# Moving a kernel's weight loads from the SyncE queue into the casting GpSimd queue, with the order of all engines planned anew

## The chip, the cores and the metric

One Trainium2 chip, one of its cores. Times are device microseconds (us) of that core; a kernel is run several times and the median is told. "Fast" runs are those in the undisturbed state. Medians here are over all runs; ratios use the fast runs alone. A profile of one execution goes with every kernel; its span is some 1.8 us below the measured time, because it leaves out start and end.

## The reference

Two parts in a row, for 8 batches of 576 tokens. First an attention with 8 heads of 64, whose keys and values are averages over 8 tokens (so 72 of them). Then four "expert" attentions with causal masks on its output `x`; a gate picks two experts for each token.

```python
# attention, for each batch and head (scale = 1/8 in both parts)
k_p = k.reshape(B, H, 72, 8, 64).mean(axis=3);  v_p = the same of v
x = softmax(scale * q @ k_p.T) @ v_p            # heads side by side: 576 x 512
# experts e = 0..3, weights wq, wk, wv: 512 x 64 each, wo: 64 x 512, w_gate: 512 x 4
logits = x @ w_gate                             # the best two of four, softmax over these two
qe, ke, ve = x @ wq[e], x @ wk[e], x @ wv[e]
ye = softmax(causal(scale * qe @ ke.T)) @ ve @ wo[e]
out += gate_weight[e] * ye                      # out: 8 x 576 x 512, fp32
```

Inputs are fp32; the kernel computes in bf16. q, k and v are 28.3 MB, the weights 2.1 MB, and the output 9.4 MB.

## The kernel before

The kernel is a list of small units (load a piece, transpose q, scores, ...), written out in one planned order, `SEQ`. A token names a unit, its step and its batch: `L` loads, `Pk`, `Pv`, `Pt` pool k and v, `Q` transposes q, `E` makes scores, `N` multiplies with v, `X` transposes x (all of the first attention); `q`, `k`, `v` project, `g` gates, `s` makes scores, `o` multiplies with v, `T` transposes and `y` projects out (experts). Each engine does its share of the list strictly in this order; only semaphores make it wait. So an engine whose next unit lacks its data waits, even if a later unit could run.

All loads of q, k and v (11 per batch) are issued by GpSimd and turn fp32 into bf16 on the way. The weights come as fp32 on SyncE's queue, and VectorE and ScalarE cast them:

```python
def load_weights():                                    # token W:0
    ...                                                # fp32 tiles wst_q, wst_k, wst_v, wst_g, wst_o
    for nm in ("q", "k", "v", "g", "o"):
        nc.gpsimd.memset(wst[nm][one element], 0.0)    # GpSimd releases SyncE at this place of the order
    for nm, src in (("q", moe_wq), ("k", moe_wk), ("v", moe_wv)):
        nc.sync.dma_start(out=wst[nm], in_=src, 128 partitions x 16 pieces of 64 elements)
    nc.sync.dma_start(out=wst["g"], ...); nc.sync.dma_start(out=wst["o"], ...)

def cast_weights(step):                                # tokens c0..c3
    if step < 2:      # q, k:  two nc.vector.tensor_copy each, fp32 -> bf16, reordered for two experts side by side
    elif step == 2:   # v and gate: two nc.vector.tensor_copy into wvg
    else:             # output weights: two nc.scalar.copy

SEQ = """
  L1:0 L9:0 L2:0 L7:0 L6:0 L4:0 M:0 L8:0 L5:0 L0:0 L3:0 L10:0 L8:1 L0:2
  I:0 Q0:0 Pk:0 Pv:0 Pt:0 L2:1 L0:1 Q1:0 ...          # I: the masks that Pk needs
  L3:2 X3:0 N1:1 E0:1 L6:2 N2:1 X1:1 L7:2 L4:2 N0:1 Pk:2 E3:1 W:0 X2:0
  L9:2 L8:2 Q1:2 Pt:2 Q2:2 Q0:2 L10:2 N3:1 E1:2 L0:3 E0:2 L3:4 E2:2 c0:0
  Q3:2 X2:1 X0:1 L2:3 X3:1 L1:3 q00:0 ...              # first projection: batch 2's attention half done
```

The softmax here doesn't subtract the row's maximum and nothing guards it: scores larger than these inputs give would overflow.

## Time and profile before

196.41 us (three runs, 195.08 to 196.64) when the prediction was made; 195.75 to 197.14 as the median of the later calls.

How to read it: TensorE (PE) is the engine with the most work. Its time is its busy time plus its idle time, so the question is where it idles. From the busy times by stretch:

| profile before, us | before 60 us | from 60 us to the last matmul | last matmul to the end | whole span |
|---|---|---|---|---|
| length | 60.0 | 125.9 | 7.5 | 193.4 |
| TensorE busy | 36.2 | 123.1 | 0 | 159.2 |
| TensorE idle | 23.8 | 2.8 | 7.5 | 34.2 |

What TensorE waited for between 25 and 60 us, in the list of waits (total us, times, longest):

```profile
PE vg_ps L319 <- DVE wvg L190: 3.5, 1, 3.5
PE qT_ps L238 <- DMA qraw_84<-in_q_dram: 2.9, 1, 2.9
PE kp_ps L387 <- DVE wkp_114 L181: 1.6, 1, 1.6
```

Two of the three are waits for weights: `wvg` and `wkp` are VectorE's cast copies. The third is batch 2's q data. And the weights' own transfers (KB, us from issue to landing), and the SyncE sequencer that issued them (start, length of the record):

```profile
wst_q<-in_moe_wq_dram SPq DMA_DIRECT2D x1, 512.0 KB, 10.5
wst_k<-in_moe_wk_dram SPq DMA_DIRECT2D x1, 512.0 KB, 16.6
wst_v<-in_moe_wv_dram SPq DMA_DIRECT2D x1, 512.0 KB, 17.9
wst_g<-in_moe_w_gate_dram SPq DMA_DIRECT2D x1, 8.0 KB, 13.0
```
```profile
27.57 0.44 SPq L165 DMA_DIRECT2D wst_q<-in_moe_wq_dram  x1
28.06 4.52 SPq L165 DMA_DIRECT2D wst_k<-in_moe_wk_dram  x1
32.62 5.69 SPq L165 DMA_DIRECT2D wst_v<-in_moe_wv_dram  x1
38.36 6.48 SPq L169 DMA_DIRECT2D wst_g<-in_moe_w_gate_dram  x1
44.88 1.19 SPq L172 DMA_DIRECT2D wst_o<-in_moe_wo_dram  x1
```

The gate weights, 8 KB, are issued last but one and land at 38.36 + 13.0 = 51.4 us; only then can the first value projection start.

### The profile page before, as it was taken

Reading aid. Unit: us, or ns where it says so; the run is one execution under the profiler, and the core shown is the slowest. Engines: PE = TensorE matmul, PEld = TensorE weight load, DVE = VectorE, ACT = ScalarE, POOL = GpSimd, SP = SyncE. Lnnn points to the kernel's source line nnn. Section 1 sums busy time; section 2 is a strip of 40 time slices with the busy share of each in tenths; the row PEclk is TensorE's granted clock in tenths of the full one; section 3 lists DMA queues with packets and bytes.
Section 4 is the critical chain, followed back from the end, with each engine's and each line's share of the span. In section 5 each row is a group of like instructions: output and inputs, shape, how many; then the busy total and the mean of one; then the engine's idle time right before and its main releaser. Section 6 shows DMA issues by size and latency. Waiting matters only on the chain.

```text
span 193.4 us, 5522 instructions
## 1 busy us (share of the span) xinstructions
PE 159.2 (82%) x2136; PEld 112.4 (58%) x2147; DVE 145.1 (75%) x558; ACT 123.9 (64%) x276; POOL 100.0 (52%) x173
## 2 busy tenths in 40 slices
PE   0009896796299999999999999999999999999940
PEld 0006463484267768685786676676777687756510
DVE  7005698675399989997799889698879877798900
ACT  2001866242666997459956968978988653989532
POOL 7999997430458799389695624010423210444000
PEclk9999999789999999999999999999999999999996
DMA  4999999999999999999999999630004110046565
GB/s 42 151 169 180 160 178 163 170 168 167 209 110 131 105 138 141 163 221 183 121 134 198 166 105 125 206 107 32 3 0 162 60 31 3 2 183 216 168 229 191
DMA packets 87404, 26.08 MB, mean 135 GB/s; under 512 B 82512, under 2 KB 82512, under 8 KB 87376
## 3 DMA queue, kind: packets, MB, share of 16 engines
q0 software_dynamic: 75136, 14.16, 88.6%
q1 hardware_dynamic: 12240, 11.55, 21.1%
q8 instruction: 17, 0.28, 0.5%
q14 instruction: 11, 0.09, 0.2%
HBM read 30.42 MB, written 9.44 MB: 206 GB/s over the span
## 4 chain that ended last, share of the span: by engine, by line
PE 44%; POOL 17%; DMA 13%; DVE 10%; ACT 7%; SPq 5%; issue 2%; DVEq 0%; POOLq 0%; ACTq 0%
DMA wst_g<-in_moe_w_gate_dram 7%; PE vg_ps L319 6%; PE oB_ps L458 6%; PE kp_ps L387 5%; SPq L165 5%; PE y_ps L500 5%; PE qp_ps L387 5%; DMA qraw_83<-in_q_dram 4%; PE sB_ps L411 4%; POOL qraw_83 L151 3%; PE xT_ps L304 3%; POOL qraw_82 L151 3%; PE oA_ps L281 2%; POOL qraw_84 L151 2%; DMA out_dram<-ofin 2%; PE sA_ps L255 2%
## 5 line engine op out<-in xcount | busy, mean ns | idle before, releaser
L442 POOL TENSOR_SCALAR_AFFINE_SELECT etb_93<-etb_93 128x256 bf16<-128x256 bf16 x32 | 12.7, 417 | 31.8 <-ACT etb_93 L429 31.8
L442 POOL TENSOR_SCALAR_AFFINE_SELECT etb_94<-etb_94 128x256 bf16<-128x256 bf16 x32 | 12.8, 416 | 30.2 <-ACT etb_94 L429 30.2
L293 DVE TENSOR_TENSOR x_tm<-oA_ps,rz 128x320 bf16<-128x320 f32 x64 | 28.2, 482 | 0.0
L429 ACT ACTIVATE etb_93<-sB_ps 128x512 bf16<-128x512 f32 x48 | 25.7, 620 | 1.3 <-PE sB_ps L411 1.3
L429 ACT ACTIVATE etb_94<-sB_ps 128x512 bf16<-128x512 f32 x48 | 25.1, 626 | 0.5 <-PE sB_ps L411 0.5
L509 ACT COPY ofin<-y_ps 128x512 f32<-128x512 f32 (+1 forms) x32 | 18.1, 597 | 10.9 <-DMA out_dram<-ofin 3.6
L270 ACT ACTIVATE eta_91<-sA_ps 96x512 bf16<-96x512 f32 x32 | 17.0, 620 | 7.8 <-PE sA_ps L255 7.8
L244 DVE COPY qT<-qT_ps 128x576 bf16<-128x576 bf16 x32 | 13.8, 451 | 6.5 <-PE qT_ps L238 5.9
L270 ACT ACTIVATE eta_92<-sA_ps 96x512 bf16<-96x512 f32 x32 | 16.6, 604 | 1.6 <-PE sA_ps L255 1.6
L151 POOL DMA_DIRECT2D qraw_82<-in_q_dram x15 | 12.9, 868 | 5.9 <-DMA vraw_90<-in_v_dram 4.6
L213 ACT CAST kp<-kp_ps 96x512 bf16<-96x512 f32 x8 | 4.8, 597 | 17.0 <-PE kp_ps L201 17.0
L304 PE MATMUL xT_ps<-ident,x_tm 128*128 128x128 bf16 x160 | 14.2, 225 | 0.7 <-DVE x_tm L293 0.5
L477 DVE TENSOR_TENSOR o_sc<-oB_ps,gt 128x320 bf16<-128x320 f32 x32 | 14.2, 484 | 0.3 <-PE oT_ps L487 0.3
L255 PE MATMUL sA_ps<-qT,kpT 64*96 64x512 bf16 (+1 forms) x128 | 14.2, 314 | 0.0
L151 POOL DMA_DIRECT2D qraw_83<-in_q_dram x15 | 12.9, 873 | 0.1
L394 ACT CAST qTB<-qp_ps 128x288 bf16<-128x288 f32 x17 | 6.8, 423 | 9.2 <-PE qp_ps L387 9.0
L304 PEld LDWEIGHTS <-x_tm 128*128 128x128 bf16 x160 | 10.8, 101 | 2.8 <-DVE x_tm L293 1.4
L319 PE MATMUL vg_ps<-wvg,xT_103 128*128 128x260 bf16 x60 | 8.4, 274 | 3.5 <-DVE wvg L190 3.5
L129 PE MATMUL one_ps<-ones,pool_111 96*32 96x8 bf16 x3 | 0.2, 188 | 12.5 <-POOL pool_111 L117 12.5
L290 DVE RECIPROCAL rz<-oA_ps 128x5 f32<-128x5 f32 x64 | 8.8, 174 | 2.1 <-PE oA_ps L281 2.0
L326 DVE CAST vaug_100<-vg_ps 128x256 bf16<-128x256 f32 x20 | 8.3, 418 | 1.7 <-PE vg_ps L319 1.7
L458 PE MATMUL oB_ps<-vaug_100,etb_94 128*128 128x65 bf16 x240 | 9.2, 193 | 0.1
(200 smaller groups left out, 441.4 us busy)
## 6 DMA issues: line engine op xcount, KB each, us to landing
out_dram<-ofin SPq DMA_DIRECT2D x32, 256.0 KB, 3.0
kraw_85<-in_k_dram POOLq DMA_DIRECT2D x9, 192.0 KB, 6.0
vraw_88<-in_v_dram POOLq DMA_DIRECT2D x9, 192.0 KB, 5.1
vraw_89<-in_v_dram POOLq DMA_DIRECT2D x9, 192.0 KB, 6.0
kraw_86<-in_k_dram POOLq DMA_DIRECT2D x9, 192.0 KB, 5.4
qraw_82<-in_q_dram POOLq DMA_DIRECT2D x12, 128.0 KB, 5.8
qraw_83<-in_q_dram POOLq DMA_DIRECT2D x12, 128.0 KB, 6.4
kraw_87<-in_k_dram POOLq DMA_DIRECT2D x6, 192.0 KB, 6.1
```

Source lines behind the costliest of these rows:

```text
L151: nc.gpsimd.dma_start(out=dst, in_=src)
L255: nc.tensor.matmul(out=s_ps[hh][:, 64 * i : 64 * i + 64] if tail else s_ps[hh][:], lhsT=kpT[r0 : r0 + D, i, :], rhs=st["qT", i][r0 : r0 + ...
L270: nc.scalar.activation(out=eta[:, hp, hh, 0:512], in_=s_ps[hh][:], func=EXP, scale=ATT_EXP_SCALE)
L293: nc.vector.tensor_tensor(out=x_tm[:, :, h * D : (h + 1) * D], in0=o_ps[hh][:, :, 0:D], in1=rz[:, hh].to_broadcast([128, NTC, D]), op=MULT,)
L304: nc.tensor.transpose(out=x_ps[:, c * 128 : (c + 1) * 128], in_=x_tm[:, c, fc * 128 : (fc + 1) * 128], identity=ident[:, :],)
L319: nc.tensor.matmul(out=vg_ps[:], lhsT=xT[:, fc, tc_ * 128 : (tc_ + 1) * 128], rhs=wvg[:, fc, :], start=(fc == 0), stop=(fc == NFC - 1),)
L387: nc.tensor.matmul(out=p_ps[:], lhsT=wqk[nm, ep][:, fc, :], rhs=xT[:, fc, cols], start=(fc == 0), stop=(fc == NFC - 1),)
L429: nc.scalar.activation(out=et[:, ep, e, eo : eo + off], in_=s_ps[e][:, 0:off], func=EXP, scale=MOE_EXP_SCALE)
L442: nc.gpsimd.affine_select(out=blk, in_=blk, pattern=[[0, 2], [1, 128]], compare_op=ISGE, fill=0.0, base=0, channel_multiplier=-1,)
L458: nc.tensor.matmul(out=o_ps[e][:, qc, :], lhsT=et[:, ep, e, col : col + 128], rhs=vaug[:, kc, 2 * ep + e, :], start=(kc == 0), stop=(kc == ...
L477: nc.vector.tensor_tensor(out=o_sc[:, :, e * HD : (e + 1) * HD], in0=o_ps[e][:, :, 0:HD], in1=gt[:, e].to_broadcast([128, NTC, HD]), op=MULT,)
L509: copy(out=ofin[0:nrows, :], in_=y_ps[0:nrows, :])
```

## The change

Its intent: the weights stand in the same GpSimd queue as the activations, behind exactly the two batches that TensorE needs first; they arrive as bf16, so VectorE only puts them in order; and the list of units is planned anew around this.

```diff
-    wop = [const.tile([128, DM], BF16, name=f"wop{ep}") for ep in range(NEP)]
+    wop = const.tile([128, NEP, DM], BF16, name="wop")
-    def load_weights():            # fp32, SyncE, released by five memsets on GpSimd
-        ...
+    wst = {nm: stp.tile([128, E, NFC, HD], BF16, ...) for nm in ("q", "k", "v")}
+    def load_weights(st, i):       # tokens W0..W4: q, k, v, gate, output weights
+        ...
+        nc.gpsimd.dma_start(out=dst, in_=src)          # fp32 -> bf16 in flight
+    def order_weights(st, i):      # tokens c0..c2: the same VectorE copies, now bf16 -> bf16; no ScalarE copies
 SEQ:
-        L1:0 L9:0 L2:0 L7:0 L6:0 L4:0 M:0 L8:0 L5:0 L0:0 L3:0 L10:0 L8:1 L0:2
-        I:0 Q0:0 Pk:0 Pv:0 Pt:0 L2:1 L0:1 Q1:0 ...
+        L2:0 L8:0 L10:0 L1:0 L6:0 L0:0 L5:0 L7:0 L3:0 L4:0 L9:0 M:0 I:0 Pk:0
+        Pt:0 Q0:0 Q1:0 Q2:0 Q3:0 E0:0 L0:1 Pv:0 L2:1 L6:1 L1:1 L3:1 E2:0 L7:1
+        E4:0 E1:0 E3:0 N2:0 L4:1 N0:0 Pk:1 L5:1 L9:1 X2:0 L8:1 L10:1 X0:0 N3:0
+        Pt:1 W0:0 W1:0 Q0:1 W2:0 W3:0 Q2:1 Q3:1 Q1:1 E0:1 X3:0 N1:0 E4:1 E3:1
+        L7:2 E1:1 Pv:1 E2:1 X1:0 c0:0 N0:1 N3:1 c1:0 N1:1 q10:0 c2:0 L2:2 L1:2
+        ...                        # first projection after batch 0 and most of batch 1; W4 much later; all the rest reordered
```

More of the change, by code (lines that the diff above doesn't have):

```diff
@@ L151, in load, with load_weights, order_weights @@
         nc.gpsimd.dma_start(out=dst, in_=src)
-    wst = {}
-    def load_weights():
-        for nm in ("q", "k", "v"):
-            wst[nm] = stp.tile([128, E, NFC, HD], FP32, name=f"wst_{nm}")
-        wst["g"] = stp.tile([128, NFC, E], FP32, name="wst_g")
-        wst["o"] = stp.tile([128, NEP, DM], FP32, name="wst_o")
-        for nm in ("q", "k", "v", "g", "o"):
-            nc.gpsimd.memset(wst[nm][0:1, 0, 0:1] if nm in "go" else wst[nm][0:1, 0, 0, 0:1], 0.0)
-        for nm, src in (("q", moe_wq), ("k", moe_wk), ("v", moe_wv)):
-            nc.sync.dma_start(
-                out=wst[nm][:].rearrange("p e fc d -> p (e fc) d"),
-                in_=src.rearrange("e (fc p) d -> p (e fc) d", p=128),
-            )
-        nc.sync.dma_start(
-            out=wst["g"][:], in_=moe_w_gate[:, :].rearrange("(fc p) e -> p fc e", p=128)
-        )
-        nc.sync.dma_start(
-            out=wst["o"][:],
-            in_=moe_wo.rearrange("e d n -> (e d) n").rearrange("(ep p) n -> p ep n", p=128),
-        )
-    def cast_weights(step: int):
-        if step < 2:
-            nm = "qk"[step]
+    wst = {nm: stp.tile([128, E, NFC, HD], BF16, name=f"wst_{nm}") for nm in ("q", "k", "v")}
+    wst_g = stp.tile([128, NFC, E], BF16, name="wst_g")
+    def load_weights(st, i: int):
+        if i < 3:
+            dst = wst["qkv"[i]][:].rearrange("p e fc d -> p (e fc) d")
+            src = (moe_wq, moe_wk, moe_wv)[i].rearrange("e (fc p) d -> p (e fc) d", p=128)
+        elif i == 3:
+            dst, src = wst_g[:], moe_w_gate.rearrange("(fc p) e -> p fc e", p=128)
+        else:
+            dst = wop[:]
+            src = moe_wo.rearrange("e d n -> (e d) n").rearrange("(ep p) n -> p ep n", p=128)
+        nc.gpsimd.dma_start(out=dst, in_=src)
+    def order_weights(st, i: int):
+        if i < 2:
+            nm = "qk"[i]
             for ep in range(NEP):
@@ L184, in cast_weights @@
                 )
-        elif step == 2:
+        else:
             nc.vector.tensor_copy(
@@ L189, in cast_weights @@
             )
-            nc.vector.tensor_copy(out=wvg[:, :, E * HD : VG], in_=wst["g"][:])
-        else:
-            for ep in range(NEP):
-                nc.scalar.copy(out=wop[ep][:], in_=wst["o"][:, ep, :])
+            nc.vector.tensor_copy(out=wvg[:, :, E * HD : VG], in_=wst_g[:])
     def pool_half(raw, nm: str):
@@ L502, in wo_out @@
                 lhsT=st["oT", ep][:, qc * 128 : (qc + 1) * 128],
-                rhs=wop[ep][:],
+                rhs=wop[:, ep, :],
                 start=(ep == 0),
@@ L516 @@
     UNITS = {
-        "L": load, "I": setup_consts, "M": setup_pads, "W": load_weights,
+        "L": load, "I": setup_consts, "M": setup_pads, "W": load_weights, "c": order_weights,
         "Pk": pool_k, "Pv": pool_v, "Pt": pool_kT, "Q": q_transposes, "E": scores_a, "N": av_a,
@@ L522 @@
     SEQ = """
-        L1:0 L9:0 L2:0 L7:0 L6:0 L4:0 M:0 L8:0 L5:0 L0:0 L3:0 L10:0 L8:1 L0:2
-        I:0 Q0:0 Pk:0 Pv:0 Pt:0 L2:1 L0:1 Q1:0 Q2:0 L1:1 Q3:0 L3:1 E0:0 L6:1
-        L4:1 E4:0 E2:0 L7:1 E1:0 N0:0 Pk:1 N2:0 L5:1 N1:0 X0:0 Pt:1 E3:0 X1:0
-        Q3:1 Q1:1 L9:1 Q0:1 L10:1 Q2:1 N3:0 E1:1 Pv:1 E4:1 L1:2 L2:2 E2:1 L5:2
-        L3:2 X3:0 N1:1 E0:1 L6:2 N2:1 X1:1 L7:2 L4:2 N0:1 Pk:2 E3:1 W:0 X2:0
-        L9:2 L8:2 Q1:2 Pt:2 Q2:2 Q0:2 L10:2 N3:1 E1:2 L0:3 E0:2 L3:4 E2:2 c0:0
-        Q3:2 X2:1 X0:1 L2:3 X3:1 L1:3 q00:0 q10d:0 L5:3 q11d:0 q01d:0 c1:0 q00d:1 q01d:1
@@ L530 @@
-        q10:1 k00d:0 k01d:0 k10d:1 k10:0 L7:3 L6:3 E4:2 L4:3 c2:0 s01:0 L3:3 E3:2 s00:0
-        v0:0 v1:0 v2:0 k11d:0 v3:0 L9:4 v4:0 s20:0 g0:0 L6:4 g1:0 L9:3 L10:3 s02:0
-        s11:0 s10:0 g2:0 Pv:2 L8:3 v0:1 v1:1 N3:2 N1:2 k00:1 L2:4 g3:0 k01:1 N0:2
-        q11:1 N2:2 L5:5 k11:1 X3:2 Pk:3 s01:1 s12:0 X1:2 L4:4 L7:4 g4:0 v2:1 L5:4
-        Pt:3 L1:5 X2:2 L10:4 v3:1 Q2:3 s20:1 g5:0 L4:5 s02:1 g6:0 g7:0 g8:0 s11:1
-        L1:4 s00:1 Q0:3 Q3:3 v4:1 X0:2 o00:0 Q1:3 L0:4 o01:0 k00d:2 c3:0 k10:2 E4:3
@@ L536 @@
-        E0:3 g0:1 s10:1 o10:0 o11:0 L8:5 q10d:2 Pv:3 E2:3 g1:1 E1:3 E3:3 T1:0 v0:2
-        v1:2 T0:0 k01d:2 N2:3 g2:1 N0:3 L4:6 L7:5 q00:2 g3:1 N3:3 k11:2 L0:5 Q0:4
-        Q2:4 L2:5 L10:5 q11:2 N1:3 L8:4 v2:2 X2:3 X3:3 y1:0 y0:0 v3:2 Pk:4 g4:1
-        s12:1 L3:6 g5:1 s12:2 g6:1 v4:2 L6:5 L5:6 g7:1 X0:3 y3:0 Q3:4 y2:0 g8:1
-        g0:2 Pt:4 o00:1 L3:5 Q1:4 g1:2 X1:3 L2:6 o10:1 o01:1 L6:6 o11:1 L1:6 E4:4
-        s11:2 Pk:5 g2:2 Pv:4 s10:2 E1:4 q01d:2 v0:3 v1:3 T1:1 L3:7 s02:2 E0:4 s00:2
-        v2:3 L9:5 g3:2 q10:3 g4:2 N1:4 g5:2 q00:3 g6:2 Q3:5 v3:3 q01:3 s20:2 L10:7
@@ L543 @@
-        s01:2 E2:4 g7:2 E3:4 L0:6 T0:1 X1:4 v4:3 Q2:5 L8:7 L5:7 g8:2 N0:4 Q0:5
-        k10d:3 N2:4 k11:3 q11:3 N3:4 y1:1 L7:7 o10:2 L7:6 Pt:5 o11:2 y0:1 L8:6 L4:7
-        Q1:5 y4:0 o00:2 L2:7 o01:2 g0:3 X3:4 Pk:6 Pv:5 L6:7 s12:3 g1:3 g2:3 E2:5
-        s11:3 X0:4 k00d:3 X2:4 T0:2 L10:6 Pt:6 k01d:3 k00:4 E4:5 E0:5 g3:3 g4:3 L1:7
-        E3:5 E1:5 Q1:6 L9:7 v0:4 Q0:6 v1:4 Q1:7 Q2:6 Q3:7 v2:4 s20:3 E0:6 s10:3
-        N1:5 T1:2 L0:7 v3:4 g5:3 N0:5 L9:6 v4:4 q10d:4 N2:5 y2:1 g6:3 y1:2 y3:1
-        q11:4 Q0:7 g0:4 s01:3 g1:4 s00:3 E1:6 Q3:6 X2:5 Q2:7 X1:5 y2:2 g7:3 N3:5
@@ L550 @@
-        k10d:4 y4:2 X0:5 k01:4 E4:6 g2:4 E3:6 g3:4 E2:6 s02:3 Pk:7 g8:3 Pv:6 Pv:7
-        o10:3 g4:4 o11:3 X3:5 y4:1 y0:2 N1:6 Pt:7 y3:2 N2:6 k11d:4 q00:4 k00:5 N0:6
-        k01:5 E3:7 E1:7 s10:4 q01d:4 N3:6 q00d:5 o00:3 o01:3 s00:4 s01:4 q10d:5 X1:6 v0:5
-        v1:5 E4:7 s12:4 s20:4 T0:3 X3:6 g5:4 k10:5 N1:7 q11:5 s02:4 E2:7 g6:4 E0:7
-        q01d:5 X2:6 v2:5 X1:7 v3:5 T1:3 X0:6 k11:5 N3:7 s00:5 s01:5 s12:5 y2d:3 y1d:3
-        q10:6 N0:7 v4:5 k00d:6 X3:7 y0:3 q11d:6 g0:5 g1:5 s20:5 g2:5 g3:5 s11:4 s02:5
@@ L556 @@
-        k01d:6 N2:7 o00:4 k10:6 y3:3 g7:4 g8:4 o01:4 g4:5 X0:7 X2:7 q00d:6 q01:6 s11:5
-        s10:5 y4:3 g5:5 q00:7 o00:5 q01:7 g6:5 T0:4 k10:7 g7:5 g8:5 o01:5 o10:4 o11:4
-        o10:5 k00d:7 k01:7 q10d:7 o11:5 v0:6 T1:4 k11d:7 q11:7 v0:7 v1:7 s00:6 s00:7 s01:7
-        v2:7 T0:5 v1:6 v3:7 s10:7 s12:7 s11:7 T1:5 k11d:6 v2:6 v3:6 y3d:5 v4:7 g0:7
-        y1d:5 s20:6 s20:7 s02:7 v4:6 g1:7 g0:6 y1d:4 g2:7 g1:6 g3:7 g4:7 y2:5 y4d:5
-        g2:6 s10:6 g5:7 g6:7 g7:7 s11:6 s12:6 g3:6 g4:6 g8:7 y0:5 o10:7 o11:7 o00:7
@@ L562 @@
-        o01:7 y0:4 y3:4 s02:6 s01:6 y2d:4 g5:6 T0:7 g6:6 T1:7 o10:6 g7:6 g8:6 o11:6
-        y4:4 y1:7 o00:6 o01:6 y4:7 y0:7 T1:6 y2:7 T0:6 y3d:7 y2:6 y0:6 y1:6 y3:6
-        y4:6
+        L2:0 L8:0 L10:0 L1:0 L6:0 L0:0 L5:0 L7:0 L3:0 L4:0 L9:0 M:0 I:0 Pk:0
[3 more added lines that the diff above has]
+        L7:2 E1:1 Pv:1 E2:1 X1:0 c0:0 N0:1 N3:1 c1:0 N1:1 q10:0 c2:0 L2:2 L1:2
@@ new lines @@
+        q00:0 L0:2 N2:1 q01:0 X0:1 X3:1 L4:2 L5:2 q11:0 k00:0 L6:2 k10:0 k01:0 k11:0
+        L3:2 v0:0 v1:0 L10:2 s20:0 s02:0 L8:2 s12:0 s11:0 X1:1 v2:0 v3:0 L7:3 v4:0
+        L9:2 X2:1 L2:3 Pk:2 s10:0 s01:0 g0:0 g1:0 s00:0 q00:1 v0:1 g2:0 Pt:2 L1:3
+        g3:0 L0:3 L4:3 Q2:2 L3:3 g4:0 v1:1 Q1:2 k00:1 Q0:2 L6:3 L5:4 L5:3 Q3:2
+        L8:3 g5:0 g6:0 q10:1 v2:1 E4:2 E2:2 g7:0 E1:2 E3:2 Pv:2 v3:1 v4:1 N2:2
+        L9:3 q01:1 N1:2 k01:1 Pk:3 E0:2 L7:4 s00:1 g8:0 s02:1 g0:1 L4:4 L10:3 X2:2
+        L1:4 k10d:1 N3:2 q11:1 g1:1 X1:2 N0:2 k11:1 L10:4 o00:0 o10:0 L0:4 X3:2 Pt:3
@@ new lines @@
+        L2:4 Q0:3 L6:4 X0:2 o11:0 g2:1 o01:0 L3:4 Q1:3 L7:5 Q3:3 v0:2 q10:2 L6:5
+        k10:2 q00d:2 k00:2 W4:0 T0:0 s20:1 s12:1 s11:1 Q2:3 q11d:2 v1:2 L2:5 v2:2 E4:3
+        E3:3 L4:5 E0:3 s10:1 Pv:3 Pk:4 v3:2 T1:0 L1:5 v4:2 N0:3 g0:2 q01:2 L5:5
+        Q3:4 g3:1 k01:2 L0:5 s01:1 L3:5 L8:4 E2:3 E1:3 L9:4 g4:1 g5:1 g1:2 Q0:4
+        Q2:4 g6:1 y4:0 X0:3 Pt:4 Q1:4 L9:5 N2:3 k11:2 L10:5 y0:0 N1:3 E4:4 s02:2
+        X2:3 N3:3 g7:1 g2:2 o00:1 g8:1 o10:1 L2:6 L3:6 X1:3 y2:0 o01:1 E3:4 L4:6
+        E2:4 L7:6 o11:1 Q3:5 L8:5 X3:3 Q1:5 Pk:5 L5:6 Pv:4 L6:6 s10:2 s00:2 L1:6
@@ new lines @@
+        E0:4 v0:3 y3d:0 Q2:5 g3:2 v1:3 q00d:3 L0:6 T1:1 L8:6 v2:3 v3:3 L10:6 s11:2
+        s12:2 E1:4 L9:6 Pt:5 k00d:3 N0:4 q10:3 y1:0 L1:7 g4:2 T0:1 N2:4 g5:2 v4:3
+        g6:2 E1:5 E2:5 X0:4 y1:1 L9:7 Q2:6 Q0:5 Q3:6 k01:3 X2:4 N3:4 k10:3 L0:7
+        L7:7 Q0:6 N1:4 s20:2 E4:5 g7:2 g0:3 g8:2 L10:7 Pk:6 Pv:5 E0:5 s01:2 E3:5
+        X1:4 Q1:6 L5:7 L2:7 g1:3 q01:3 Pt:6 N2:5 y2:1 g2:3 X3:4 k11:3 g3:3 N0:5
+        g4:3 q11:3 X2:5 E4:6 E1:6 E3:6 L6:7 N1:5 o00:2 o01:2 q10:4 X1:5 o10:2 k10:4
+        o11:2 s20:3 g5:3 L4:7 s12:3 s01:3 v0:4 N3:5 y4:1 X0:5 T1:2 L3:7 v1:4 s10:3
@@ new lines @@
+        s11:3 s00:3 T0:2 k11:4 g6:3 v2:4 y0:1 g7:3 X3:5 v3:4 Pv:6 Pk:7 s02:3 E2:6
+        L8:7 E0:6 q11:4 q00d:5 Q1:7 v4:4 g0:4 Q3:7 N3:6 q00:4 g8:3 N2:6 y3:1 o10:3
+        q01:4 o00:3 o01:3 Pt:7 k00:5 o11:3 y4:2 X2:6 g1:4 k00:4 k01d:4 N1:6 y1:2 Q2:7
+        s10:4 E1:7 N0:6 Q0:7 X3:6 q10:5 k10:5 X1:6 E4:7 s01:4 E2:7 g2:4 s02:4 g3:4
+        Pv:7 X0:6 T0:3 v0:5 y2d:2 T1:3 q01:5 v1:5 s11:4 s12:4 g4:4 E3:7 v2:5 g5:4
+        g6:4 k01:5 N1:7 v3:5 y1d:3 g7:4 v4:5 y3:2 k11:5 s20:4 g0:5 E0:7 s00:4 g1:5
@@ new lines @@
+        s01:5 q10d:6 q11:6 q11d:5 k00d:6 g2:5 N3:7 q00:6 N0:7 y3d:3 y4d:3 y2:3 k10:6 o10:4
+        g8:4 o00:4 g3:5 N2:7 o11:4 q01:6 o01:4 y0:2 v0:6 s02:5 s10:5 y0d:3 k11:6 T0:4
+        v1:6 s11:5 s00:5 s12:5 X3:7 g4:5 T1:4 v2:6 k01:6 g5:5 v3:6 X1:7 g6:5 g7:5
+        y4:4 v4:6 y1:4 y2:4 g0:6 X2:7 g1:6 X0:7 g2:6 s20:5 g8:5 s02:6 s12:6 s10:6
+        o00:5 k00:7 g3:6 y3d:4 o01:5 o10:5 o11:5 g4:6 k10:7 q00:7 v0:7 s01:6 s11:6 s00:6
+        g5:6 v1:7 v2:7 v3:7 T0:5 q01d:7 v4:7 k01:7 q10d:7 T1:5 s20:6 s01:7 g0:7 s02:7
@@ L565 @@
+        s00:7 o00:6 g6:6 g1:7 g7:6 g8:6 g2:7 g3:7 o01:6 q11:7 g4:7 o10:6 g5:7 g6:7
+        o11:6 k11:7 y3:5 y0d:4 s20:7 s11:7 g7:7 s12:7 s10:7 y1d:5 g8:7 T1:6 T0:6 y4d:5
+        y2:5 o00:7 y1:6 o01:7 y0:6 o10:7 o11:7 y4:6 y0:5 y2:6 T0:7 T1:7 y3:6 y2:7
+        y0:7 y1:7 y3:7 y4:7
     """
@@ L576 @@
             copy = nc.vector.tensor_copy if on_dve else nc.scalar.copy
-            if name in "IMW":
+            if name in "IM":
                 UNITS[name]()
-            elif name == "c":
-                cast_weights(int(digits))
             elif name == "L":
```

## The prediction

> **What bounds the kernel now.** The profile's first part gives TensorE 159.2 us busy of a 193.4 us span. The busy times by stretch put its 34.2 us of idleness in three places: 23.8 us in the first 60 us (14.3 of them before 20 us), 2.5 us between 60 and 180 us, 7.8 us after 180 us. In the middle TensorE is 98% busy, so nothing but less TensorE idleness at the two ends can help much. The timeline shows the head: the first matmul on q data waits until 14.5 us; batch 0 and 1 then run until about 35 us with gaps for data; the first projection starts at 40.1 us; the key projection waits for its weights until 45.3 us and the value projection until 51.9 us (the waits list has VectorE waiting 2.1 us for the k weights and 3.2 us for v; TensorE then waits 1.6 and 3.5 us for VectorE's casts). The weights were asked for only at 27.6 us, on the SyncE queue, and took 10.5, 16.6 and 17.9 us from issue to landing for 512 KB each, gate 13.0 us, in competition with the activation loads. The DMA row is full and the rate some 170 GB/s (counted in bf16) from 5 to 50 us, so the loads are limited by rate there, not by latency.
>
> **What the change does.** The four projection weights enter the casting GpSimd queue after exactly two batches of loads (22 transfers), and batch 2, of which the old order had already issued much, comes after them. Trainium skill, "DMA: Bandwidth & Descriptors", section "SWDGE vs HWDGE vs iDMA": only the GpSimd path casts in flight; so half the bytes land, and VectorE only reorders bf16. The same page ("Issuing engines are not separate DMA queues") says all issuers share the 16 engines: the gain is order, not a new path. Removed: five tiny memsets, two 0.69 us ScalarE casts, none critical. Added on GpSimd: five issues; from 0.69, 0.77 and 0.88 us for 512, 768 and 1024 pieces I estimate 1.3 us for a 2048-piece weight, 5 us in all. VectorE's five or six reorderings stay near 0.4 us each. TensorE's work is unchanged.
>
> **Estimate.** Two batches are 3.54 MB as bf16: at 170 GB/s, landed at about 25 us; q, k, v, gate weights (0.79 MB) by about 30-31 us instead of 50.6. GpSimd's masks come after 11 issues instead of 13, and pooled k is first on TensorE, so it starts near 11.5 us. Before the first projection the new order has only batches 0 and 1 of attention, some 14 us of TensorE work; the first projection should start near 30 us, so about 16 us idle by then. After it, the rest of both batches (about 30 us of work) covers batch 2's loads. With 2 to 3 us of small stalls the first 60 us cost 18 to 19 us of idleness instead of 23.8. The middle and the tail (still 11 stores bunched behind four output buffers, 7.5 us after the last matmul) I expect unchanged within 1.5 us. Gain about 5.5 us: 191 us, range 187 to 194.8. Chances: faster by over 2% 0.68, within 2% 0.28, slower 0.04.
>
> **Signs.** Right: value projection starts at 32-36 us; weight waits gone; TensorE idle under 20 us in the first 60; TensorE busy sum within 1.5 us of 159; tail 7 to 8 us. Wrong step: weight landings after 36 us, or batch 1 data late by as much.
>
> **What would make it wrong.** The 128-byte weight pieces moving well below 170 GB/s; the new order stalling TensorE in mid-kernel (idle 60-180 us above 5 us); a longer tail; or batch 2's data arriving after the covering work is used up.

## More of the kernel before

The stretches from which the head is read (columns: start and end, length, busy us and instructions of PE, PEld, DVE, ACT and POOL, the TensorE clock that was granted, as a share of full speed, the DMA share, which is the summed time of the packets over that of 16 engines and passes 1 where packets overlap, and GB/s):

```profile
0.00:60.00 60.00, 36.16 (x423) 24.42 (x424) 35.47 (x128) 24.29 (x52) 41.42 (x67) 0.97 1.68 155
30.00:35.00 5.00, 2.12 (x30) 1.24 (x29) 3.00 (x11) 2.24 (x5) 3.87 (x5) 1.00 1.84 166
35.00:40.00 5.00, 4.72 (x52) 3.63 (x53) 4.19 (x12) 2.47 (x6) 1.69 (x3) 0.66 1.49 171
45.00:50.00 5.00, 3.08 (x32) 1.94 (x32) 2.43 (x7) 2.54 (x7) 0.54 (x2) 1.00 1.60 165
```

TensorE works only 2.12 of the 5 us from 30 us; just after this its granted clock is 0.66. DMA moves 165 GB/s (counted as it lands, in bf16 where cast) all the time.

## The result, and the profile after

183.99 us (four runs, 183.62 to 185.82) beside 195.75 us before. The ratio is 0.9427 (95% interval 0.933 to 0.952); ratios here are the mean time of one kernel's fast runs over that of the other's of the same rounds, so not quite the ratio of the medians. A later repeat of the same kernel (e14) gave 184.05 us and 0.9344. The gain is 11.8 us, about twice the predicted 5.5, and the time lies below the predicted range.

The stretches of the new kernel:

```profile
0.00:60.00 60.00, 43.38 (x569) 30.75 (x570) 39.51 (x159) 31.44 (x71) 50.41 (x75) 1.00 1.75 138
30.00:35.00 5.00, 4.90 (x76) 4.08 (x74) 4.97 (x21) 3.61 (x9) 2.79 (x4) 1.00 2.24 165
35.00:40.00 5.00, 5.00 (x56) 3.85 (x54) 4.13 (x15) 3.98 (x12) 2.51 (x6) 1.00 1.65 121
45.00:50.00 5.00, 4.83 (x64) 3.22 (x62) 3.86 (x16) 4.20 (x11) 5.00 (x7) 1.00 1.69 161
```

From 30 us on TensorE hardly idles, and the dip of its clock is gone. The waits for weights are gone from the list of waits between 25 and 60 us; the largest that is left:

```profile
PE sA_ps L244 <- DVE qT L233: 0.6, 1, 0.6
```

And the weights, whose GpSimd issues start at 21.2 us:

```profile
wst_q<-in_moe_wq_dram POOLq DMA_DIRECT2D x1, 256.0 KB, 8.0
wst_k<-in_moe_wk_dram POOLq DMA_DIRECT2D x1, 256.0 KB, 8.5
wst_v<-in_moe_wv_dram POOLq DMA_DIRECT2D x1, 256.0 KB, 9.7
wst_g<-in_moe_w_gate_dram POOLq DMA_DIRECT2D x1, 4.0 KB, 8.9
```

The gate weights are there at 24.58 + 8.9 = 33.5 us instead of 51.4. Up to 30 us nothing was gained (TensorE idle 15.5 us before, 15.8 after); the head's whole gain lies between 30 and 60 us. Where TensorE's time went, in the profiled executions (a matmul count below 2147 means that records are missing from that trace, and the busy time is then a little too low and the idle time too high):

| us | span | busy | matmuls seen | idle before 60 | idle 60 to last matmul | last matmul to end |
|---|---|---|---|---|---|---|
| before | 193.4 | 159.2 | 2136 | 23.8 | 2.8 | 7.5 |
| after | 181.9 | 157.0 | 2130 | 16.6 | 1.5 | 6.8 |
| after, repeat (e14) | 181.4 | 158.5 | 2147 | 15.6 | 0.6 | 6.8 |
| e1: old order, casting queue | 186.4 | 159.3 | 2147 | 17.3 | 3.1 | 6.7 |
| e3: new order, SyncE queue | 193.5 | 162.9 | 2147 | 22.2 | 0.9 | 7.5 |
| e4: new order, weights late | 192.9 | 162.4 | 2147 | 21.9 | 1.6 | 7.0 |

Between before and the repeat, which has all its records: 8.2 us less idle in the head, 2.2 in the middle, 0.7 in the tail, and 0.8 busy; 12.0 us together. The head is most of it.

### The profile page after: what moved, and what is told of

It reads as the page before. It is cut to its first block, busy times and chain, and to the rows that moved or that the text cites. A ratio compares the mean times of both kernels' runs of the same rounds, so it can differ in the third digit from the quotient of the medians.

```text
span 181.9 us, 5531 instructions
## 1 busy us (share of the span) xinstructions
PE 157.0 (86%) x2130; PEld 111.5 (61%) x2147; DVE 137.0 (75%) x541; ACT 128.9 (71%) x291; POOL 105.2 (58%) x173
## 4 chain that ended last, share of the span: by engine, by line
PE 62%; DMA 12%; POOL 10%; ACT 9%; DVE 4%; issue 2%; ACTq 0%; POOLq 0%
PE oB_ps L447 8%; PE vg_ps L308 7%; PE kp_ps L376 7%; PE qp_ps L376 7%; PE y_ps L489 6%; PE sB_ps L400 5%; PE oA_ps L270 4%; PE xT_ps L293 4%; DMA qraw_82<-in_q_dram 4%; PE sA_ps L244 4%; PE qT_ps L227 4%; DMA kraw_86<-in_k_dram 3%; DMA kraw_85<-in_k_dram 3%; ACT etb_93 L418 3%; POOL qraw_82 L151 2%; POOL kraw_85 L151 2%
## 5 line engine op out<-in xcount | busy, mean ns | idle before, releaser
L418 ACT ACTIVATE etb_93<-sB_ps 128x512 bf16<-128x512 f32 x48 | 25.0, 613 | 2.1 <-PE sB_ps L400 2.0
L418 ACT ACTIVATE etb_94<-sB_ps 128x512 bf16<-128x512 f32 x48 | 25.0, 622 | 0.4 <-PE sB_ps L400 0.4
L383 ACT CAST qTB<-qp_ps 128x288 bf16<-128x288 f32 x24 | 9.9, 418 | 8.0 <-PE qp_ps L376 7.7
L244 PE MATMUL sA_ps<-qT,kpT 64*96 64x64 bf16 (+1 forms) x128 | 13.7, 312 | 0.6 <-DVE qT L233 0.6
L151 POOL DMA_DIRECT2D qraw_83<-in_q_dram x15 | 12.8, 866 | 0.3 <-issue 0.3
L151 POOL DMA_DIRECT2D qraw_82<-in_q_dram x15 | 12.8, 870 | 0.0
L151 POOL DMA_DIRECT2D qraw_84<-in_q_dram x10 | 8.8, 887 | 3.2 <-DMA wst_v<-in_moe_wv_dram 1.4
L447 PEld LDWEIGHTS <-etb_94 128*128 128x128 bf16 x240 | 8.7, 97 | 2.2 <-issue 0.6
```

The costliest lines, as they stand in the source:

```text
L151: nc.gpsimd.dma_start(out=dst, in_=src)
L244: nc.tensor.matmul(out=s_ps[hh][:, 64 * i : 64 * i + 64] if tail else s_ps[hh][:], lhsT=kpT[r0 : r0 + D, i, :], rhs=st["qT", i][r0 : r0 + ...
L418: nc.scalar.activation(out=et[:, ep, e, eo : eo + off], in_=s_ps[e][:, 0:off], func=EXP, scale=MOE_EXP_SCALE)
L447: nc.tensor.matmul(out=o_ps[e][:, qc, :], lhsT=et[:, ep, e, col : col + 128], rhs=vaug[:, kc, 2 * ep + e, :], start=(kc == 0), stop=(kc == ...
```

## The experiments

Sixteen runs were made, e1 to e16, all with correct results. The theories: *arrival* (the gain is the earlier arrival of the weights), *order* (the replanned order makes it, the path is only its vehicle), and within arrival *queue* (which queue the weights stand in) against *cast* (half the bytes, cheaper reorderings); later also *clock* (gaps cost a slow stretch after them).

**e1: the old order, only the weight path changed.**

```diff
 (the new kernel's code, with the old SEQ:)
-  ... Pk:2 E3:1 W:0 X2:0 ...
+  ... Pk:2 E3:1 W0:0 W1:0 W2:0 W3:0 W4:0 X2:0 ...      and without c3:0
```

> Old written order, only the weight path changed: the five weight transfers go through the casting GpSimd queue at the very place where the old order asked SyncE for them (27.6 us), bf16 reorderings in place of casts. Arrival theory (the gain is the weights' arrival, whatever brings it): q, k, v, gate land at about 35, 36, 38, 38 us instead of 38, 45, 50 and 51; the waits of 1.6 us (k) and 3.5 us (v) on TensorE vanish; time 190 to 191.5 us, about 5 us under the old kernel. Order theory (the replanned order makes the gain, the path is only its vehicle): within 2 us of the old kernel.

Measured: 187.91 us beside 196.4, ratio 0.955; again as e15 187.52 us, 0.9495. So the path alone, at the old place, gives 8.5 to 9.6 us. The arrival theory holds, and I had the size of this too low as well. Both waits for weights vanished; the wait for batch 2's q data fell from 2.9 to 1.5 us too, and is now the largest between 25 and 60 us:

```profile
PE qT_ps L227 <- DMA qraw<-in_q_dram: 1.5, 1, 1.5
```

3.5 + 1.6 + 1.4 = 6.5 us, and idle before 60 us fell by as much, from 23.8 to 17.3. (The two profiled spans differ by 7.0 us, 0.9 of it in the tail; the rest of the 8.5 us lies in the spread between runs.)

**e2: the same, with the four projection weights moved forward to the new kernel's place in the queue.**

```diff
-  ... L10:1 ...      ... W0:0 W1:0 W2:0 W3:0 W4:0 ...
+  ... L10:1 W0:0 W1:0 W2:0 W3:0 ...     ... W4:0 ...
```

> As the run before, and the q, k, v and gate weights are moved forward to just behind batch 1's last load (about 21 us), the place they have in the new kernel; everything else in the old order. TensorE's old order does nearly all of batch 2's attention before the first projection, and batch 2's data now comes some 4.5 us later. Arrival theory: weights land by 31 us, but TensorE then waits for batch 2's q data (2.9 us already in the old trace), so no better than the run before, 190 to 193 us: early weights are worth something only if TensorE's order uses them. Order theory in its strict form: no gain over the old kernel.

Measured: 194.46 us, ratio 0.990, just above the 190 to 193 that the arrival theory expected. Earlier weights are 6.5 us slower than later ones here: TensorE's old order wants batch 2's attention before the first projection, and batch 2 now stands behind the weights. TensorE's two largest waits between 25 and 60 us are for its data:

```profile
PE kp_ps L190 <- DMA kraw<-in_k_dram: 2.5, 1, 2.5
PE qT_ps L227 <- DMA qraw<-in_q_dram: 1.4, 1, 1.4
```

In 35 to 45 us the granted clock is 0.50 and 0.64.

**e3: the new order, with the old fp32 path on SyncE.**

```diff
-  ... Pt:1 W0:0 W1:0 Q0:1 W2:0 W3:0 ...   ... W4:0 ...
+  ... Pt:1 W:0 Q0:1 ...                   ... c3:0 ...       old load_weights and cast_weights
```

> New written order on all engines, old weight path: fp32 through SyncE asked for at the place of the new kernel's first weight transfer (about 21 us), with the old casts on VectorE and ScalarE. Arrival theory: from the old 10.5, 16.6 and 17.9 us to landing and the serial issue on SyncE, q lands at about 32, k at 38, v at 44 us; TensorE idles some 6 to 8 us more than in the new kernel before 60 us: 190 to 192 us. Order theory: at most 186 us.

Measured: 195.88 us beside 196.4, ratio 0.9989 (0.992 to 1.006). The new order alone is worth nothing. The weights landed as expected (31.8, 37.4 and 43.4 us), yet the time is 4 us above the expected 190 to 192; the profile shows TensorE 4.4 us busier than in the new kernel's repeat, in part in stretches of half clock. Its first projections come where the weights are not yet there; the two largest waits between 12 and 60 us:

```profile
PE vg_ps L319 <- DVE wvg L190: 4.8, 1, 4.8
PE qp_ps L387 <- DVE wqp L181: 2.9, 1, 2.9
```

**e4: the new kernel with batch 2's eleven loads in front of the weights.**

```diff
-  ... Pt:1 W0:0 W1:0 ...
+  ... Pt:1 L7:2 L2:2 L1:2 L0:2 L4:2 L5:2 L6:2 L3:2 L10:2 L8:2 L9:2 W0:0 W1:0 ...
```

> The new kernel with batch 2's eleven loads moved in front of the weights in the GpSimd queue; nothing else changes. Arrival theory: 1.77 MB more at about 165 GB/s ahead of the weights, so they land some 10 us later (39 to 44 us instead of 29 to 33.5), and TensorE's order has nothing to do in between: idle up to 9 us more in the first 60 us, 191 to 193 us. Order theory: 184 to 186 us.

Measured: 193.38 us, ratio 0.986, against 191 to 193 expected. Same path, same cast, same order on TensorE, VectorE and ScalarE: only the weights' place in GpSimd's queue, behind batch 2's loads, differs, and 9.4 of the 11.8 us are lost. TensorE waits 8.1 us for the q weights. Together, e1 to e4 show that place and order must fit each other.

**e5: the old kernel, its fp32 weights issued by GpSimd instead of SyncE.** No cast in flight, same place, same casts on VectorE and ScalarE.

```diff
-            nc.sync.dma_start(out=wst[nm], ...)
+            nc.gpsimd.dma_start(out=wst[nm], ...)            (all five)
```

> The old kernel with one change: its five fp32 weight transfers are issued by GpSimd instead of SyncE, at the same place, without a cast in flight; the old casts on VectorE and ScalarE stay. Tells the queue from the cast. If the gain of the first run (old order, casting queue: 187.9 us) comes from the weights standing in line in the one GpSimd queue instead of sharing the engines piecewise from a second queue: 187.5 to 189.5 us. If it comes from the halved bytes and cheaper reorderings: 192 us or more.

Measured: 187.81 us beside 196.6, ratio 0.952 (one of the four runs, 190.08 us, is slow; the median of the other three is 187.25). One word, the issuing engine, makes the whole gain of e1. The transfers and their issue:

```profile
wst_k<-in_moe_wk_dram POOLq DMA_DIRECT2D x1, 512.0 KB, 8.9
wst_v<-in_moe_wv_dram POOLq DMA_DIRECT2D x1, 512.0 KB, 11.2
```
```profile
29.00 1.16 POOL L165 DMA_DIRECT2D wst_k<-in_moe_wk_dram  x1
30.15 1.16 POOL L165 DMA_DIRECT2D wst_v<-in_moe_wv_dram  x1
```

The same bytes of k and v, with the same shapes, landed 8.9 and 11.2 us after issue instead of 16.6 and 17.9, and were issued at 29.0 and 30.2 us instead of 28.1 and 32.6. The wait for batch 2's q data, 2.9 us before, is 0.8 us here:

```profile
PE qT_ps L238 <- DMA qraw<-in_q_dram: 0.8, 1, 0.8
```

In the old kernel loads that nobody needed yet shared the rate with the weights. Batch 3's k loads, issued from 30.9 us on, took this long to land beside the SyncE transfers:

```profile
DMA to landing us min/median/max: 13.5/16.4/17.3
```

From 35 to 45 us of that profile the GpSimd queue moved 3724 packets and the SyncE queue 3345, together 168 GB/s. In one queue what is asked for first comes first. The Trainium skill, "DMA: Bandwidth & Descriptors", section "Queues, rings and completion order", says that each DMA engine goes round the rows that have work, packet by packet; the two nearly equal counts fit that, without proving it. Its section "Issuing engine by pattern" says that the SyncE kind of queue "is generally faster"; in this pair of runs, beside a full GpSimd queue, it was slower.

**e6: the new order, SyncE path, asked for 10 us earlier.**

```diff
-  ... L4:0 L9:0 M:0 I:0 ...           ... Pt:1 W:0 ...
+  ... L4:0 L9:0 W:0 M:0 I:0 ...       ... Pt:1 ...
```

> New order, old fp32 SyncE path, asked for at about 10 us (behind batch 0's loads) instead of 21 us. Arrival theory: landing about 10 us sooner than in the run with the SyncE path at 21 us, so q by 22, k by 27, v and gate by 33 us, before TensorE wants them; batch 1's loads share the rate meanwhile and come up to 4 us later; 185 to 189 us against 195.9. If SyncE's path itself is the trouble, it stays above 192 us.

Measured: 195.32 us, ratio 0.994: the plain form of the arrival theory failed. The weights did land before they were wanted (gate at about 35 us, first projection after 40). But batch 1's loads now shared the rate with all five weights, and TensorE waited for them instead; the granted clock is 0.50 to 0.60 from 25 to 40 us:

```profile
PE kp_ps L201 <- DMA kraw<-in_k_dram: 6.3, 2, 5.3
PE qT_ps L238 <- DMA qraw<-in_q_dram: 3.4, 3, 2.2
```

So the theory that stands is not "earlier" but: what is landed at each time must be what the order wants next, and a second queue in parallel spoils this for both. How much of e6's loss is the second queue's and how much the early place's is not shown: no run put the weights at 10 us into GpSimd's queue.

**e7 and e10: filling the wait of e4.** 34, then 42 dummy matmuls on a constant tile in front of the first projection. They move no data.

```diff
+    w_ps = p1.tile([128, 512], FP32, ...)
+    for _ in range(42): nc.tensor.matmul(out=w_ps[:], lhsT=wz[:, 0:128], rhs=wz[:], start=True, stop=True)
-  ... N1:1 q10:0 ...
+  ... N1:1 F42:0 q10:0 ...
```

> The new kernel with late weights (193.4 us, TensorE waiting 8.1 us and then at half clock for over 4 us), with 34 dummy 512-column matmuls on a constant tile (7.3 us of work) put in front of the first projection, in the wait. They move no data and do nothing useful. Clock theory [...]: the first eight projection matmuls take 1.14 us instead of 2.10, and time falls by about 2 us, to 191 to 192. Without it: no change, or slower.

> Repeats the run with the wait for late weights filled by dummy matmuls, with 42 instead of 34: there 2.3 us of the wait stayed open and the clock still fell. 42 take 9.1 us, to about 39.9 us, where the weights come. Clock theory: first eight projection matmuls 1.14 to 1.2 us, granted clock 1.00 from 40 to 45 us, 191 to 192.5 us against 193.4 unfilled. Rival (the slow stretch costs nothing at the end, or the filler delays as much as it saves): 193 to 195 us.

Measured: 195.12 us (e7; the weights came later than the filler lasted, 2.3 us stayed open, and the clock still fell) and 194.44 us (e10), beside 193.38 unfilled. In e10 the mechanism worked and the time did not follow. The stretches of e4 and of e10 from 35 to 45 us (columns as above; the clock stands third from the end):

```profile
35.00:40.00 5.00, 0.86 (x4) 0.58 (x5) 1.41 (x6) 0.00 (x0) 0.00 (x0) 0.50 2.43 157
40.00:45.00 5.00, 5.00 (x42) 3.95 (x40) 4.72 (x19) 1.81 (x5) 0.00 (x0) 0.64 0.28 13
```
```profile
35.00:40.00 5.00, 4.81 (x24) 2.05 (x22) 0.69 (x5) 0.00 (x0) 0.00 (x0) 1.00 2.39 156
40.00:45.00 5.00, 4.35 (x44) 2.97 (x43) 5.00 (x19) 1.77 (x5) 0.00 (x0) 1.00 0.42 18
```

And the first eight projection matmuls of e4, then of e10:

```profile
39.14 2.10 PE L376 MATMUL qp_ps<-xT,wqp 128*128 128x288 bf16 x8 [8.12 <-DVE wqp L173]
```
```profile
39.86 1.29 PE L376 MATMUL qp_ps<-xT,wqp 128*128 128x288 bf16 x8 [0.19 <-DVE wqp L173]
```

The clock stayed at 1.00 and they took 1.29 instead of 2.10 us. Yet in e10 VectorE was busy for all of 40 to 45 us, TensorE waited for it, and the first value projection began at 46.09 us against 46.05. In e10 the first projection began 0.7 us later and this was made up. So here the half rate after a gap lay under another limit and its removal bought nothing that can be measured (the ratios, 0.991 and 0.986, have overlapping intervals, and the 191 to 192.5 us of the clock theory did not come); the 4 us by which e3 and e4 are busier than the repeat cannot simply be added to their loss. The Trainium skill, "TensorE: Matmul & The Clock Gate", Part 1, says that the clock falls to half after an idle window of about 3.4 us or more; here it fell after gaps of 2.9 us (before), 2.5 us (e9) and 2.3 us (e7), but not after the old kernel's gap of 3.5 us before its first value projection (clock 1.00 from 50 to 55 us). So the length of a gap alone does not decide, and what does is not shown.

**e8 and e16: the new kernel with 36 dummy matmuls in TensorE's idle first 12 us.**

```diff
-  ... L4:0 L9:0 M:0 I:0 Pk:0 ...
+  ... L4:0 L9:0 F0:0 F36:0 M:0 I:0 Pk:0 ...              (F0 sets the constant tile)
```

> The new kernel with 36 dummy 512-column matmuls in TensorE's idle first 12 us. Clock theory: the first real matmuls (pooled k, q transposes, scores) run at full rate, 0.61 instead of 1.04 us for pooled k and 1.28 instead of 2.2 us for the q transposes; but q's data lands only at 16 us and batch 1's later, so of the 3 us saved on TensorE about 1 us reaches the end: 182.5 to 183.5 us beside 184.0.

> The new kernel with 36 dummy matmuls in TensorE's idle first 12 us, once more: clock theory 182 to 183 us, at least 1 us under the new kernel beside it; if the earlier 1.6 us was the spread between calls, within 0.7 us of it.

Measured: e8 182.38 us, ratio 0.929 (0.923 to 0.935); e16 183.7 us, ratio 0.9292, beside 184.05 and 0.9344 for the new kernel on the same chip, with overlapping intervals. The 0.35 us between these medians is within the 0.7 us that e16 had set for mere spread. (The clock column cannot be used here: the traces of before and after hold no clock record before some 20 us, and the column shows 1.00 there.) In the profile of e8 pooled k took 0.61 us and the nineteen q transposes 1.23 us, against 1.04 and 2.21 in the new kernel; in that of e16 the clock had fallen again in the gaps up to 16 us, and these nineteen took 1.77 us. Three of its six runs, with mean clocks of 0.99 (two) and 0.986, took 181.8 to 183.4 us, three at 0.97 to 0.98 about 184 to 184.7. A gain of up to one and a half us is possible; it is not shown.

**e9 and e13: fp32 through GpSimd's queue, in the new order.**

```diff
 e9:  -  nc.sync.dma_start(fp32 weights)   +  nc.gpsimd.dma_start(...) at the new kernel's places; casts on VectorE,
         and on ScalarE for the output weights, just before y4:0
 e13: the same for q, k, v and gate only; output weights cast in flight
```

> The new kernel's order with fp32 weights issued by GpSimd at the new kernel's places (output weights late), and the old casts on VectorE and ScalarE. Separates queue from cast in the new order too. Queue theory: the fp32 bytes cost GpSimd's queue perhaps 2 us more before batch 2's loads, VectorE's casts 0.15 us more each; within 1.5 us of the new kernel: 184 to 185.5 us. Cast theory: 188 us or more.

> As the fp32 run in the new order, but only the q, k, v and gate weights come as fp32 through GpSimd's queue and are cast on VectorE; the output weights come cast in flight, as in the new kernel, so ScalarE has no casts. Queue theory: the wait of 2.5 us for the output weights vanishes, 184.5 to 186 us, within 2 us of the new kernel beside it. Cast theory: still 188 us or more.

Measured: e9 189.75 us, which looked as if the cast mattered. But its head is as good as the new kernel's (first value projection at 36.7 us against 36.4). The loss is at 72 us, and it is my edit's: ScalarE's casts of the output weights stood behind four exponentials, and TensorE waited for them:

```profile
PE y_ps L501 <- ACT wop L194: 2.5, 1, 2.5
```

e13 took that out: 184.92 us, ratio 0.939 (0.935 to 0.944), beside 184.05 and 0.934 (0.930 to 0.939) for the new kernel. So in the new order too it is the queue: e3, with the same order, nearly the same place (first issue at 20.4 and 20.8 us) and the same fp32 q, k, v and gate weights on SyncE (the output weights too), took 195.88. The cast in flight of these and their bf16 copies are worth 0.9 us by the medians; the intervals overlap, so this is not clear of zero; from their outer ends I estimate at most some 3 us.

**e11 and e12: eight output buffers instead of four, without and with the warm start.**

```diff
-    ofp = ... tile_pool(name="ofp", bufs=4)
+    ofp = ... tile_pool(name="ofp", bufs=8)
```

> The new kernel with eight instead of four output buffers. In its last 7 us ScalarE's copies wait 1.6 us for a store to free a buffer, behind a last matmul at 175.1 us. If the buffers hold the tail up: last copy about 1.5 us earlier and 183.0 to 183.5 us. If the stores' rate (some 270 GB/s at the end) does: 183.8 to 184.3 us.

> Both additions at once: 36 dummy matmuls in the first 12 us and eight output buffers, on the new kernel. If they add up: 181.3 to 182.3 us, against 182.4 with the warm start alone and 184.0 for the new kernel.

Measured: 183.43 us, ratio 0.934 (e11), and 182.49 us, ratio 0.925 with a wide interval (0.911 to 0.938; e12). In e11 ScalarE's wait for stores is gone and its last copy ends at 175.2 us instead of 178.7; but the span ends 6.4 us after the last matmul instead of 6.8. By the expected ranges 183.43 us would speak for the buffers, but the ratio is the new kernel's own (0.934) and the tail only 0.4 us shorter, so the buffers hold at most little of it. That the stores' rate holds it is not shown (294 GB/s from 170 to 175 us and 205 after it, 291 and 212 in the new kernel). The two additions do not add up to the expected 181.3 to 182.3 us: e12 is not clearly faster than e8.

**e14, e15, e16: five rounds side by side on one chip.**

> The new kernel itself, once more, as the mark for the other three on this chip: 183.5 to 185 us.

> The old order with the casting GpSimd queue, once more: if the new order adds to the new path, 187 to 189 us and above the new kernel beside it by 3 to 4 us with intervals apart; if it does not, within 1.5 us of it.

Measured: new kernel 184.05 us (0.930 to 0.939), old order with the casting queue 187.52 us (0.945 to 0.954). The intervals are apart: the new order adds some 3 us to the new path (3.5 by the medians, 3.0 by the ratios). One of e15's six runs, the profiled one, took 316.95 us; its matmuls ran at about half rate throughout (TensorE busy 296.9 us). It is not used in the ratio, and its cause is open; its trace holds no clock record. No kernel was found that surely beats the new one.

## Why the prediction was wrong

The direction, the places and most signs were right; the size was not. Three steps failed: the 2 to 3 us of stalls, the middle and tail held unchanged, and the clause "order, not a new path".

- *What bounds the kernel: TensorE idleness in the first 60 us.* Right: of 12.0 us between the profiles of before and of the repeat, 8.2 are there.
- *Weights land at 30 to 31 us, first projection near 30 us.* Nearly: the last landed at 33.5 us, and the first projection began at 31.6 us. The arrival was 2.5 to 3.5 us later than estimated and cost nothing, since TensorE had batch 1's rest to do. The value projection came at 36.4 us, just outside the stated 32 to 36.
- *"With 2 to 3 us of small stalls the first 60 us cost 18 to 19 us of idleness instead of 23.8."* This is the step that failed first. It was 16.6 us (15.6 in the repeat): in the profile after, 15.8 us up to 30 us, as predicted, and only 0.9 after it (15.1 and 0.5 in the repeat). The stalls that I added for safety did not come.
- *"Batch 0 and 1 then run until about 35 us with gaps for data."* Among these gaps is the wait of 2.9 us for batch 2's q data, which I took as the price of a full DMA rate. e5 shows it was largely the weights' own doing: it fell to 0.8 us when the same fp32 bytes stood in GpSimd's queue. This did not enter the sum; but of the old waits I laid only 1.6 + 3.5 = 5.1 us to the weights' path, and e1 showed 6.5 us of head idleness and 8.5 us in time.
- *"The gain is order, not a new path."* This clause failed as a mechanism, though half of it holds. The two queues did share one rate (168 GB/s together from 35 to 45 us), and place in the queue decides (e4 loses 9.4 us by place alone). But the queue from which a transfer is issued did matter: e5 gains 8.8 us by it with no new order of transfers written, and e3, order without queue, gains nothing; on top of the path the order adds some 3 us (e14, e15). The expectation of e1, 190 to 191.5 us, repeated this mis-sizing.
- *"The middle and the tail I expect unchanged within 1.5 us."* Together 2.0 us better (10.3 to 8.3), in the repeat 2.9. Part of the middle's 2.8 us before may be missing records, but e1, with all its records and the old order, has 3.1 us there and the repeat 0.6. So in these profiles the replanned order gained in the middle as well; 1.2 us of e1's is a wait for a late q load near 103 us.
- *TensorE busy within 1.5 us of 159.* The profile said 157.0, but with 17 matmuls missing; the complete repeat says 158.5. Right.

Summed up: head 8.2 for 5.3, middle and tail 2.9 for 0, busy 0.8 for 0. The range of 187 to 194.8 us was placed around a sum in which each term was on the low side. What stays open: whether the SyncE path was slow through the sharing alone or also through slow issue (three of its five records were open for 4.5 to 6.5 us), since e5 changes both.

## What to carry to other kernels

When urgent and non-urgent loads are in flight together, try them in one queue in the order in which they will be wanted; here a second queue shared the rate between them (e5), and asking earlier on it only moved the wait to other data (e6). Here the replanned order was worth nothing without the arrival that it assumes (e3) and some 3 us with it (e14, e15): test each alone before crediting either. And a slow-clock stretch or a busy time is a cost only where that engine is what the next wait ends on; count it in the time, not in the busy sum.

## What the Trainium skill lacked or had wrong

- "DMA: Bandwidth & Descriptors", section "Issuing engine by pattern", calls the SyncE kind of queue generally faster. For fp32 weights in 256-byte pieces beside a full GpSimd queue it was slower: k and v 16.6 and 17.9 us to landing from SyncE, 8.9 and 11.2 us from GpSimd (e5), and 8.8 us of kernel time.
- The same page, section "Issuing engines are not separate DMA queues", says that issuing from several engines only saves the sequencer's time. It lacks the harm: beside weights from a second issuing engine, batch 1's loads (e6, up to 16.0 us) and batch 3's k loads (before, up to 17.3 us) took long to land, where 192 KB of k takes 6.0 us in the median.
- The same section calls the time to initiate a DMA "usually small relative to the DMA itself". In the old kernel three of SyncE's five issue records were open for 4.5 to 6.5 us while the DMA engines were busy, the longest for the 8 KB of the gate, and one of 512 KB for only 0.44 us; GpSimd's records of 512 KB (e5) took 1.16 us. Whether SyncE's were issuing or waiting is not shown.
- "TensorE: Matmul & The Clock Gate", Part 1, gives an idle window of 3.4 us or more for the fall to half rate, and elsewhere gaps of about 3 us. Here the clock fell after a gap of 2.3 us (e7, 0.66 from 40 to 45 us) and did not after one of 3.5 us (before, 1.00 from 50 to 55 us). That such a stretch may cost nothing measurable I found on no page: e10 removed it and was not faster (194.4 us against 193.4).
